# Three places of their own for the combined token operands, and a later ready time for them in the planner

## The chip, the core and the metric

One core of one Trainium2 chip runs the whole program. A core has TensorE (PE, matrix products into PSUM), VectorE (DVE), ScalarE (ACT), GpSimd (POOL) and SyncE (SP, which issues the transfers). The metric is the device time of one execution in microseconds (us), as a median of runs. All values are float32 at the interface.

## What is computed

```python
def reference(**kwargs):
    ...
    attn_out = _attn_ref(**attn_kwargs)     # two rounds of softmax attention over 4 x 8 heads, 576 tokens
    x = ...                                 # 2304 tokens x 512
    x = _moe_ref(x=x, **moe_kwargs)         # g = h*clip(h+3,0,6)/6 with h = x @ w_in;  g @ w_out
    return _moe2_ref(x=x, **moe2_kwargs)

def _moe2_ref(x, w_gate, w1, w2):
    ...
    for _ in range(8):                      # 8 rounds of row and column normalisation of P (2304 x 8)
        ...
    for e in range(E):                      # 8 experts
        h = np.maximum(x @ w1[e], 0.0)      # 512 -> 1024
        ye = h @ w2[e]                      # 1024 -> 512
        out += P[:, e:e + 1] * ye
```

The second mixture, `_moe2_ref`, takes three quarters of the time, and the change lies there.

## The kernel before, in words

**Stages.** 0 to about 140 us attention; then the first mixture (`layer1a`, `layer2a`); from about 375 to 525 us the gate and the normalisation of P (lines L1111 to L1190, small DVE instructions); the second mixture from about 440 us to the end. In the second mixture the 2304 tokens are six blocks of 384 (TB). A pair of blocks goes through all 32 groups of expert columns. The first pair (blocks 0 and 1) is pass 0, to about 944 us; the other two pairs share each group's weights in one long pass, from about 944 to 1946 us.

**Precision.** A float32 value is fed to TensorE as a high and a low part. `split_part` makes them: ACT copies the high part (L424), and the low part is the difference `x - high`, one tensor_tensor (L429) that may run on DVE or POOL. A product is three matmuls for each contraction chunk: high by high (L992), low by high (L993), high by low (L994).

**A unit** of the second mixture is one pair of token blocks and one group of columns. `layer1b` computes a 2 by 2 block product with seven products in place of eight. Its token operands a11, a12, a22, s1, s2, s3, s4 are made once for a pair by `operands` (L945): s1 = a21+a22, s2 = s1-a11, s4 = a12-s2, s3 = a11-a21 (L969, on DVE or POOL, for two halves c each), and each is then split. Its weight operands are made for each group by `combined` (L431): four differences of the raw weights (`m`, L451), and splits of them and of the raw weights: `w1h`, `w1l` and `w1xh`, `w1xl` (128x256 or 128x512 pieces). The weights of layer 2 are split whole: `w2h` on ACT and `w2l` (128x1024) on DVE or POOL.

Each product is six matmuls into a PSUM bank `ph`, about 1.04 us. A product's PSUM value is copied into a temporary `tmp` by ACT (L300) or DVE (L301), and DVE adds the next products to it with L1006, `u.t = ps.t + u.t`. In the order of a unit: a11 (copied), s3 (copied), s2 (copied into u2), a22, **L1006 (u2 += a22)**, s1, **L1006 (p7 += s1)**, a12, L1006 (p1 += a12), s4. The product s4 goes into the bank that s1 was in, so it waits until L1006 (p7 += s1) has read it. Then ACT applies relu (L1014), and the result is split into `hsh` (ACT, L424) and `hsl` (L429, DVE or POOL). `layer2b` (L1051 to L1053) follows in six groups of twelve matmuls into banks `po`, 1.36 us each, and DVE adds each to the output (L1075), times the share Pr. TensorE interleaves the units: part of the seven products of one unit stand beside products of the next unit, and layer 2 of the unit before stands between.

**What sets the order.** Nothing is issued in the order of the code. Every operation goes into a list scheduler (`Order`) that walks through the whole kernel before it is built. An operation has ways (engine and modelled cost), tiles that it holds, dependencies and a priority. `run` picks the operation that can start first, gives it the engine on which it ends first, and moves that engine's clock. The queues of the engines are what comes out. A tile needs a free place of its tag (`Res`): `place(tag, pool, count, late)` gives the count of places, and `late` is how many come on top for the second mixture. The model prices a DVE or POOL instruction by its columns alone, whatever the other engine does.

The result of an operation is ready for others at `o.end = start + cost + o.lat` plus 0.2 us; `lat` is 2.0 for transfers and otherwise 0. Operations with `lat` 0 and a priority of 100 or more have 0.2 us (PATIENCE) added in the comparison.

```python
    place("hs", hp, 3)
    place("tmp", hp, 2, 4)
```

The order that comes out is thus sensitive: a different free place or ready time at one operation moves those after it, on all engines, until the end of the program.

Of the kernel before, what the change touches and what calls it, by code (L numbers as in the profile page):

```python
# [133 lines left out]
def t_dve(n, fast=False):  # L134
    return 0.065 + n / (1920.0 if fast else 960.0)
# [6 lines left out]
def t_pool(n):  # L142
    return 0.15 + n / 465.0
# [7 lines left out]
def tile_kernel(  # L151
# [21 lines left out]
    E, _, F2 = moe2_w1.shape  # L173
# [6 lines left out]
    TB = 384  # L180
# [8 lines left out]
    def pool(name, stack=ctx, **kw):  # L189
        return stack.enter_context(tc.tile_pool(name=name, bufs=1, **kw))  # L190

    const, dp, accp, hp, wp = (pool(n) for n in ("const", "dp", "accp", "hp", "wp"))
# [8 lines left out]
    def place(tag, where, count, late=0):  # L201

        res[tag] = Res(count)
        res[tag].pool, res[tag].first, res[tag].late = where, count, late
# [20 lines left out]
        pieces[tag] += 1  # L225
        return tag if pieces[tag] % (len(res[tag].free_at) + len(extra)) < len(res[tag].free_at) else tag + "_early"
    place("hs", hp, 3)
    place("tmp", hp, 2, 4)
    place("ph", ph, 2, 2)
    place("po", ph, 2, 2)  # L230
    for j in range(NB):
# [33 lines left out]
    def maker(tag, shape, dt, parts):  # L265
        def make(i):
            r = res[tag]
            pool = r.pool if i < r.first else r.late_pool if i < r.first + r.late or not r.late else r.last_pool
            got = [pool.tile(shape, dt, tag=f"{tag}{x}_{i}", name=f"{tag}{x}_{i}") for x in parts]
            return got if len(parts) > 1 else got[0]  # L270

        return make

    def hold(tag, shape, dt=F32):
        return Hold(res[tag], maker(tag, shape, dt, ("",)))
# [30 lines left out]
    def alt(cost_dve, cost_pool, fn, spare=0.0, **kw):  # L306

        return order.op(
            [
                ("POOL", cost_pool, lambda: fn(nc.gpsimd)),  # L310
                ("DVE", cost_dve, lambda: fn(nc.vector), spare),
            ],
            **kw,
        )
# [106 lines left out]
    def split_part(dst, src, w, n, deps, prio, **kw):  # L421

        high = act(
            t_act(n), lambda: nc.scalar.activation(dst(w.t[0]), src(), AF.Copy),  # L424
            reads=deps, fills=[w], prio=prio, **kw,
        )
        return alt(
            t_dve(n), t_pool(n),
            lambda e: e.tensor_tensor(dst(w.t[1]), src(), as_f32(dst(w.t[0])), ALU.subtract),  # L429
            reads=deps, fills=[w], after=[high], prio=prio, spare=SPARE,  # L430
        )  # L431
# [50 lines left out]
    def operand():  # L482
        late = maker("xy", [128, KC // 2, TB], F32R, ("h", "l"))
        return Hold(
            res["xy"], lambda i: parts(two_of[i // 3], (i % 3) * KC * TB, (KC // 2, TB)) if i < 6 else late(i)
        )
# [336 lines left out]
    def tmp():  # L823
        return hold("tmp", [128, TB])
# [120 lines left out]
    def operands(pr, prio, after=lambda nth: ()):  # L945


        a, b = acc[2 * pr], acc[2 * pr + 1]
        o = {nm: operand() for nm in ("a11", "a12", "a22", "s1", "s2", "s3", "s4")}
        turn = {nm: after(n) for n, nm in enumerate(("a11", "a12", "a22", "s1", "s2", "s4", "s3"))}  # L950
        for nm, src, c0 in (("a11", a, 0), ("a12", a, 2), ("a22", b, 2)):
            for c in range(2):
                split_part(
                    lambda d, c=c: d[:, c, :], lambda src=src, c=c, c0=c0: src.t[:, c0 + c, :], o[nm], TB, [src],
                    prio - (nm == "a11"), after=turn[nm],
                )
        for c in range(2):
            s1, s2, s3, s4 = (tmp() for _ in range(4))
            a11, a12 = (lambda c=c: a.t[:, c, :]), (lambda c=c: a.t[:, 2 + c, :])
            a21, a22 = (lambda c=c: b.t[:, c, :]), (lambda c=c: b.t[:, 2 + c, :])  # L960
            for nm, s, i0, i1, how, deps in (
                ("s1", s1, a21, a22, ALU.add, [b]),
                ("s2", s2, lambda s1=s1: s1.t, a11, ALU.subtract, [s1, a]),
                ("s4", s4, a12, lambda s2=s2: s2.t, ALU.subtract, [a, s2]),
                ("s3", s3, a11, a21, ALU.subtract, [a, b]),
            ):
                alt(
                    t_dve(TB), t_pool(TB),
                    lambda e, s=s, i0=i0, i1=i1, how=how: e.tensor_tensor(s.t, i0(), i1(), how),  # L969
                    reads=deps, writes=[s], takes=[o[nm]], after=turn[nm], prio=prio,  # L970
                )
                split_part(
                    lambda d, c=c: d[:, c, :], lambda s=s: s.t, o[nm], TB, [s], prio
                )
        return o
# [232 lines left out]
    with tc.manual_schedule():  # L1208
# [25 lines left out]
        for gg in range(4):  # L1234
# [7 lines left out]
            writes=[wg], prio=90,  # L1242
# [21 lines left out]
        for blk in range(NB):  # L1264
            gate(blk)
        ops = {0: operands(0, 40)}
        routing()
        i = len(units)
        turn, done = 100 + G1, []
        for ps in passes:  # L1270
            for pr in ps:
                if pr not in ops:
                    ops[pr] = operands(
                        pr, 45 if pr > 1 else 200, lambda n, pr=pr: [done[-1] if pr > 1 else done[4 + 3 * n]]
                    )
            gs = list(range(G1, len(groups)))
            turns_of = [(gs[:2], pr) for pr in ps] + [([g], pr) for g in gs[2:] for pr in ps]
            ready = {}
            for some, pr in turns_of:
                for g in some:  # L1280
                    if g not in ready:
                        ready[g] = (*combined(g, turn), whole(g, "w2", turn, "w2"))
                        turn += 1
                for g in some:
                    wa, wb, w2 = ready[g]
                    hs = [pair("hs", [128, NFC, TB]) for _ in range(2)]
                    done.append(layer1b(i, ops[pr], wa, wb, hs))
                    for h in (1, 0):
                        layer2b(i, g, 2 * pr + h, w2, hs[h])
                    i += 1  # L1290
# [33 lines left out]
```

## Time and profile before

| | |
|---|---|
| time, median of 3 runs | 1957.03 us (1956.8 to 1957.29) |
| profiled execution, its own time | 1953.73 us, of which 1951.9 us are the profile's span |
| PE busy | 1915.4 us (98%) |
| DVE busy | 1208.9 us (62%) |
| ACT busy | 970.3 us (50%) |
| POOL busy | 947.6 us (49%) |

In the profile, L12 is line 12 of the kernel, and `out<-in` are tile names without their numbers. A timeline row is a start, a length, engine, line, operation and tiles; in square brackets stands how long the engine was idle before and what released it. "xN" at the end of a timeline row means N like instructions in a row, with their joint length. PE's rows overlap, since matmuls are pipelined: the next one starts while the last one is still shown. PEclk is the granted clock of TensorE as a share of 2.4 GHz.

### The profile page before, as it was taken

How to read it: one execution, taken by the hardware profiler on the slowest of the kernel's cores; microseconds unless marked ns; L12 is line 12 of the kernel's file. 1: busy time of each engine (PE TensorE's matmuls, PEld its weight loads, DVE VectorE, ACT ScalarE, POOL GpSimd, SP SyncE). 2: the span in 40 equal slices, each digit the busy share in tenths (PEclk: the TensorE clock that was granted, in tenths of full speed). 3: DMA queues.
4: the chain of work that ended last, by engine and by line, in shares of the span. 5: the costliest groups of instructions: out<-in, count | busy, mean ns of one | idle time of the engine just before them, and what ended most of it. 6: DMA issues, size and time to landing. Idle time of an engine off the chain costs nothing.

```text
span 1951.9 us, 28194 instructions
## 1 busy us (share of the span) xinstructions
PE 1915.4 (98%) x10573; PEld 1735.5 (89%) x10573; DVE 1208.9 (62%) x1998; ACT 970.3 (50%) x2135; POOL 947.6 (49%) x987
## 2 busy tenths in 40 slices
PE   6999999999999999999999999999999999999998
PEld 4789999999899989999899999999999999999997
DVE  6996686447866676666755655555555555555554
ACT  6885674335455555555554443444443344443432
POOL 2444675236665666656634544435344343444431
PEclk9999999999999999999999999999999999999999
DMA  9931121001222222222311101111110111101102
GB/s 212 190 91 33 51 70 44 11 1 44 66 65 72 69 65 76 65 65 65 87 33 33 44 22 44 33 33 33 33 44 33 33 33 33 44 22 44 33 11 66
DMA packets 103546, 104.87 MB, mean 54 GB/s; under 512 B 42736, under 2 KB 78576, under 8 KB 103408
## 3 DMA queue, kind: packets, MB, share of 16 engines
q1 hardware_dynamic: 103408, 103.06, 19.5%
q8 instruction: 83, 1.36, 0.3%
q14 instruction: 55, 0.45, 0.1%
HBM read 98.32 MB, written 4.72 MB: 53 GB/s over the span
## 4 chain that ended last, share of the span: by engine, by line
PE 91%; DVE 5%; ACT 1%; DMA 1%; issue 0%; POOL 0%; SPq 0%; DVEq 0%; ACTq 0%; POOLq 0%
PE po L1051 13%; PE po L1052 13%; PE po L1053 13%; PE ph L992 12%; PE ph L994 12%; PE ph L993 12%; PE po L924 3%; PE po L926 3%; PE po L925 3%; PE ph L886 2%; PE ph L888 1%; PE ph L887 1%; PE ph L837 1%; DMA k<-in_k_dram 1%; DVE m_early L344 0%
## 5 line engine op out<-in xcount | busy, mean ns | idle before, releaser
L1075 DVE SCALAR_TENSOR_TENSOR acc<-po,Pr,acc 128x512 f32<-128x512 f32 x504 | 377.2, 750 | 287.3 <-PE po L1053 284.0
L429 POOL TENSOR_TENSOR hsl<-tmp,hsh 128x384 fp32r<-128x384 f32 x382 | 392.5, 1032 | 325.2 <-ACT hsh L424 271.0
L1051 PE MATMUL po<-w2h,hsh 128*128 128x512 f32 x1152 | 448.9, 390 | 0.0
L1052 PE MATMUL po<-w2l,hsh 128*128 128x512 f32 x1152 | 448.7, 390 | 0.0
L1053 PE MATMUL po<-w2h,hsl 128*128 128x512 f32 x1152 | 448.6, 389 | 0.0
L429 POOL TENSOR_TENSOR w1xl<-m,w1xh 128x256 fp32r<-128x256 f32 x152 | 111.5, 756 | 321.6 <-ACT w1xh L424 321.6
L1053 PEld LDWEIGHTS po<-w2h,hsl 128*128 128x128 f32 x1152 | 216.2, 188 | 45.2
L300 ACT ACTIVATE tmp<-ph 128x384 f32<-128x384 f32 x241 | 117.9, 489 | 274.6 <-PE ph L994 263.3
L1051 PEld LDWEIGHTS po<-w2h,hsh 128*128 128x128 f32 x1152 | 216.3, 188 | 41.7 <-DVE acc L1075 0.2
L1052 PEld LDWEIGHTS po<-w2l,hsh 128*128 128x128 f32 x1152 | 216.3, 188 | 41.5
L424 ACT ACTIVATE hsh<-tmp 128x384 fp32r<-128x384 f32 x480 | 242.4, 520 | 20.2 <-DVE tmp L904 12.4
L1006 DVE TENSOR_TENSOR tmp<-ph,tmp 128x384 f32<-128x384 f32 x288 | 159.8, 556 | 147.3 <-PE ph L994 129.7
L424 ACT ACTIVATE w2h<-raw 128x1024 fp32r<-128x1024 f32 x64 | 67.9, 1061 | 350.2 <-PE po L1053 338.2
L1014 ACT ACTIVATE tmp<-tmp 128x384 f32<-128x384 f32 x288 | 149.7, 520 | 87.6 <-DVE tmp L1006 83.2
L992 PE MATMUL ph<-ax,w1h 128*128 128x384 f32 x448 | 151.5, 338 | 3.3 <-DVE tmp L1006 3.3
L994 PE MATMUL ph<-ax,w1l 128*128 128x384 f32 x448 | 150.7, 336 | 0.0
L993 PE MATMUL ph<-ax,w1h 128*128 128x384 f32 x448 | 150.5, 336 | 0.0
L429 DVE TENSOR_TENSOR hsl<-tmp,hsh 128x384 fp32r<-128x384 f32 x98 | 106.0, 1082 | 42.0 <-ACT hsh L424 38.5
L429 POOL TENSOR_TENSOR w1l<-raw,w1h 128x512 fp32r<-128x512 f32 (+1 forms) x104 | 116.1, 1130 | 7.0 <-ACT w1h L424 5.9
L451 POOL TENSOR_TENSOR m<-raw 128x256 f32<-128x256 f32 x58 | 44.5, 770 | 139.1 <-DMA raw<-in_moe_w_dram 136.3
L992 PE MATMUL ph<-xyh,w1h 128*128 128x384 f32 x320 | 108.3, 339 | 3.7 <-ACT tmp L300 3.7
L993 PE MATMUL ph<-xyl,w1h 128*128 128x384 f32 x320 | 108.1, 338 | 0.0
(207 smaller groups left out, 4035.7 us busy)
## 6 DMA issues: line engine op xcount, KB each, us to landing
raw<-in_moe_w_dram SPq DMA_DIRECT2D x128, 512.0 KB, 3.5
raw<-in_moe_w_in_dram SPq DMA_DIRECT2D x16, 512.0 KB, 3.8
raw<-in_moe_w_out_dram SPq DMA_DIRECT2D x16, 512.0 KB, 3.6
k<-in_k_dram SPq DMA_DIRECT2D x32, 144.0 KB, 5.9
q<-in_q_dram SPq DMA_DIRECT2D x32, 144.0 KB, 4.6
v<-in_v_dram SPq DMA_DIRECT2D x8, 576.0 KB, 6.7
out_dram<-acc SPq DMA_DIRECT2D x36, 128.0 KB, 2.4
p<-in_p_dram SPq DMA_DIRECT2D x1, 224.0 KB, 5.4
```

The source lines that it names most:

```text
L300: ("ACT", t_act(n, True), lambda: nc.scalar.activation(dst(), src(), AF.Copy)),
L424: t_act(n), lambda: nc.scalar.activation(dst(w.t[0]), src(), AF.Copy),
L429: lambda e: e.tensor_tensor(dst(w.t[1]), src(), as_f32(dst(w.t[0])), ALU.subtract),
L992: nc.tensor.matmul(out, wh[:, at + c, :], bh[:, c, :], start=first and c == 0, **on)
L993: nc.tensor.matmul(out, wh[:, at + c, :], bl[:, c, :], start=False, **on)
L994: nc.tensor.matmul(out, wl[:, at + c, :], bh[:, c, :], start=False, **on)
L1006: t_dve(n), lambda: nc.vector.tensor_tensor(u.t, ps.t[:, :n], u.t, ALU.add),
L1014: t_act(n, bool(ps)), lambda: nc.scalar.activation(c.t, src(), AF.Relu),
L1051: nc.tensor.matmul(ps.t, hh[:, f, ts], wh[:, f, :], start=(f == 0), stop=False)
L1052: nc.tensor.matmul(ps.t, hh[:, f, ts], wl[:, f, :], start=False, stop=False)
L1053: nc.tensor.matmul(ps.t, hl[:, f, ts], wh[:, f, :], start=False, stop=(f == NFC - 1))
L1075: lambda row=row, share=share, ps=ps: nc.vector.scalar_tensor_tensor(row(), ps.t, share(), row(), ALU.mult, ALU.add),
```

## The change

The six places of `tmp` in the second mixture become three, and three places with a new tag `st` are made; `operands` takes the combinations s1 to s4 from `st`. The four combinations carry `lat=2.0`, so the planner believes that they end 2 us later than they do.

```diff
     place("hs", hp, 3)
-    place("tmp", hp, 2, 4)
+    place("tmp", hp, 2, 1)
+    place("st", None, 0, 3)
     place("ph", ph, 2, 2)
...
         for c in range(2):
-            s1, s2, s3, s4 = (tmp() for _ in range(4))
+            s1, s2, s3, s4 = (hold("st", [128, TB]) for _ in range(4))
...
                 alt(
                     t_dve(TB), t_pool(TB),
                     lambda e, s=s, i0=i0, i1=i1, how=how: e.tensor_tensor(s.t, i0(), i1(), how),
-                    reads=deps, writes=[s], takes=[o[nm]], after=turn[nm], prio=prio,
+                    reads=deps, writes=[s], takes=[o[nm]], after=turn[nm], prio=prio, lat=2.0,
                 )
```

From the place of the diff on, line numbers of the changed kernel are one higher (L429 becomes L430, L1006 becomes L1007). No instruction of TensorE is added or removed. The queues of all engines are the same up to about 390 us. From there on, the order differs. DVE has 1973 rows in place of 1985, ACT 2117 in place of 2093, POOL 981 in place of 990.

On DVE, one unit of pass 0 (the one whose product a22 starts at 598.25 us in the trace of before; the numbers in a name are its place and a serial number). Before:

```order
L1075 SCALAR_TENSOR_TENSOR acc0_0_5526<-po_1_6889,Pr_0_5509,acc0_0_5526 128x512
L429 TENSOR_TENSOR w2l_0_6913<-raw_0_6833,w2h_0_6912 128x1024
L1006 TENSOR_TENSOR tmp_0_6931<-ph_2_6903,tmp_0_6931 128x384
L1006 TENSOR_TENSOR tmp_2_6922<-ph_0_6820,tmp_2_6922 128x384
L1006 TENSOR_TENSOR tmp_4_6844<-ph_3_6948,tmp_4_6844 128x384
L301 COPY tmp_3_6992<-ph_1_6971 128x384
L429 TENSOR_TENSOR hsl_0_6982<-tmp_1_6979,hsh_0_6981 128x384
```

Now:

```order
L1076 SCALAR_TENSOR_TENSOR acc0_0_5535<-po_1_6927,Pr_0_5522,acc0_0_5535 128x512
L1007 TENSOR_TENSOR tmp_0_6879<-ph_3_6835,tmp_0_6879 128x384
L430 TENSOR_TENSOR w1xl_1_6953<-m_1_6904,w1xh_1_6952 128x256
L1007 TENSOR_TENSOR tmp_2_6865<-ph_2_6809,tmp_2_6865 128x384
L430 TENSOR_TENSOR w1xl_1_6953<-m_0_6905,w1xh_1_6952 128x256
L430 TENSOR_TENSOR hsl_1_6968<-tmp_0_6879,hsh_1_6967 128x384
L430 TENSOR_TENSOR w1l_1_7003<-raw_1_6869,w1h_1_7002 128x512
```

The wide split `w2l` that stood ahead of the first L1006 has left DVE, and a split `w1xl` now stands between L1007 (u2 += a22) and L1007 (p7 += s1). This pattern comes 14 times in pass 0 now.

On POOL, the same unit now:

```order
L430 TENSOR_TENSOR hsl_2_6892<-tmp_1_6830,hsh_2_6891 128x384
L452 TENSOR_TENSOR m_1_6904<-raw_1_6869,m_2_6903 128x256
L430 TENSOR_TENSOR w2l_0_6943<-raw_0_6806,w2h_0_6942 128x1024
L430 TENSOR_TENSOR hsl_1_6968<-tmp_2_6865,hsh_1_6967 128x384
L430 TENSOR_TENSOR hsl_2_6892<-tmp_0_6991,hsh_2_6891 128x384
```

Here the wide split `w2l` stands, which needs `w2h` from ACT. And on ACT, the same unit now:

```order
L425 ACTIVATE w2h_0_6942<-raw_0_6806 128x1024
L425 ACTIVATE w1xh_1_6952<-m_1_6904 128x256
L425 ACTIVATE w1xh_1_6952<-m_0_6905 128x256
L1015 ACTIVATE tmp_0_6879<-tmp_0_6879 128x384
L425 ACTIVATE hsh_1_6967<-tmp_0_6879 128x384
```

`w2h` stands right ahead of the two `w1xh`, the first of which the first `w1xl` on DVE needs.

On DVE, where pass 0 ends and the operands of blocks 4 and 5 are made, the rows ahead of L1006 (p7 += s1), which is the last row of each piece. Before:

```order
L1075 SCALAR_TENSOR_TENSOR acc0_0_5526<-po_2_10432,Pr_0_5509,acc0_0_5526 128x512
L969 TENSOR_TENSOR tmp_0_10458<-acc5_0_3007 128x384
L969 TENSOR_TENSOR tmp_4_10468<-acc4_0_2867,acc5_0_3007 128x384
L1075 SCALAR_TENSOR_TENSOR acc0_0_5526<-po_3_10446,Pr_0_5509,acc0_0_5526 128x512
L969 TENSOR_TENSOR tmp_3_10484<-tmp_0_10458,acc4_0_2867 128x384
L429 TENSOR_TENSOR w1xl_1_10311<-m_1_10268,w1xh_1_10310 128x256
L1006 TENSOR_TENSOR tmp_1_10486<-ph_2_10352,tmp_1_10486 128x384
L969 TENSOR_TENSOR tmp_0_10502<-acc4_0_2867,tmp_3_10484 128x384
L1006 TENSOR_TENSOR tmp_2_10374<-ph_1_10339,tmp_2_10374 128x384
```

Now:

```order
L1076 SCALAR_TENSOR_TENSOR acc1_0_5569<-po_0_10413,Pr_0_5522,acc1_0_5569 128x512
L430 TENSOR_TENSOR ax0_94<-st_2_10387,ax0_94 128x384
L1076 SCALAR_TENSOR_TENSOR acc0_0_5535<-po_1_10430,Pr_0_5522,acc0_0_5535 128x512
L430 TENSOR_TENSOR w1l_1_10383<-raw_1_10240,w1h_1_10382 128x512
L970 TENSOR_TENSOR st_0_10466<-st_2_10387,acc4_0_2867 128x384
L1076 SCALAR_TENSOR_TENSOR acc0_0_5535<-po_2_10444,Pr_0_5522,acc0_0_5535 128x512
L1076 SCALAR_TENSOR_TENSOR acc0_0_5535<-po_3_10459,Pr_0_5522,acc0_0_5535 128x512
L970 TENSOR_TENSOR st_2_10493<-acc4_0_2867,st_0_10466 128x384
L1007 TENSOR_TENSOR tmp_0_10490<-ph_1_10352,tmp_0_10490 128x384
L430 TENSOR_TENSOR ax1_95<-st_0_10466,ax1_95 128x384
L1007 TENSOR_TENSOR tmp_2_10373<-ph_0_10340,tmp_2_10373 128x384
```

Before, four combinations (L969) and a `w1xl` stand among the last rows ahead of that L1006. Now it is two combinations, two splits `ax` of operands and a `w1l`, and the last accumulations of layer 2 stand closer to it.

## Rows read from the trace of the kernel before

**Rows 1.** The page, part 1: busy us (share of the span) xinstructions of each engine.

```profile
PE 1915.4 (98%) x10573; PEld 1735.5 (89%) x10573; DVE 1208.9 (62%) x1998; ACT 970.3 (50%) x2135; POOL 947.6 (49%) x987
```

**Rows 2.** Windows: per engine busy us (and matmul count), PEclk, DMA share, GB/s.

```profile
530.00:944.00 414.00, 414.00 (x2087) 375.53 (x2086) 281.08 (x407) 223.41 (x480) 256.04 (x274) 1.00 0.23 69
...
970.00:1946.00 976.00, 976.00 (x4919) 886.29 (x4919) 526.74 (x771) 413.08 (x878) 405.76 (x412) 1.00 0.12 34
```

**Rows 3.** Timeline of PE at its three waits after 460 us: start, length, [idle before <-releaser].

```profile
489.20 0.45 PE L992 MATMUL ph<-ax,w1h 128*128 128x384 f32 x1 [0.76 <-DVE tmp L1006]
...
526.05 0.45 PE L992 MATMUL ph<-ax,w1h 128*128 128x384 f32 x1 [2.52 <-DVE tmp L1006]
...
959.16 0.69 PE L992 MATMUL ph<-xyh,w1h 128*128 128x384 f32 x1 [3.66 <-ACT tmp L300]
```

**Rows 4.** Timeline of PE, one unit of pass 0: first matmul of its 1st and 4th product and of two layer-2 groups.

```profile
583.84 0.34 PE L992 MATMUL ph<-ax,w1h 128*128 128x384 f32 x1
...
586.96 0.34 PE L992 MATMUL ph<-ax,w1h 128*128 128x384 f32 x1
...
588.00 0.39 PE L1051 MATMUL po<-w2h,hsh 128*128 128x512 f32 x1
...
589.37 0.39 PE L1051 MATMUL po<-w2h,hsh 128*128 128x512 f32 x1
```

**Rows 5.** Timelines of ACT, DVE and POOL in the same unit.

```profile
584.04 1.06 ACT L424 ACTIVATE w2h<-raw 128x1024 fp32r<-128x1024 f32 x1 [0.59 <-PE po L1053]
...
585.08 0.56 DVE L1006 TENSOR_TENSOR tmp<-ph,tmp 128x384 f32<-128x384 f32 x1 [0.29 <-PE ph L994]
586.12 0.56 DVE L1006 TENSOR_TENSOR tmp<-ph,tmp 128x384 f32<-128x384 f32 x1 [0.48 <-PE ph L994]
...
585.18 2.42 POOL L429 TENSOR_TENSOR w2l<-raw,w2h 128x1024 fp32r<-128x1024 f32 x1 [0.89 <-ACT w2h L424]
```

**Rows 6.** Timelines of POOL and DVE: a vector instruction under a wide split, and one alone.

```profile
721.33 2.67 POOL L429 TENSOR_TENSOR w2l<-raw,w2h 128x1024 fp32r<-128x1024 f32 x1 [0.87 <-ACT w2h L424]
...
721.85 2.44 DVE L451 TENSOR_TENSOR m<-raw,m 128x256 f32<-128x256 f32 x1
...
670.18 0.41 DVE L429 TENSOR_TENSOR w1xl<-m,w1xh 128x256 fp32r<-128x256 f32 x1
```

**Rows 7.** Timelines of POOL and DVE before the wait at 488 us.

```profile
486.26 2.40 POOL L429 TENSOR_TENSOR w2l<-raw,w2h 128x1024 fp32r<-128x1024 f32 x1 [1.68 <-PE ph L1181]
...
487.07 1.62 DVE L1187 TENSOR_SCALAR ct<-ct 128x8 f32<-128x8 f32 x1
488.60 0.55 DVE L1006 TENSOR_TENSOR tmp<-ph,tmp 128x384 f32<-128x384 f32 x1
```

**Rows 8.** Timelines of POOL and DVE where a vector instruction isn't stretched.

```profile
458.51 1.44 POOL L429 TENSOR_TENSOR hsl<-tmp,hsh 128x384 fp32r<-128x384 f32 x1 [0.24 <-ACT hsh L424]
...
458.67 0.40 DVE L451 TENSOR_TENSOR m<-raw 128x256 f32<-128x256 f32 x1
```

**Rows 9.** Lines by shape, DVE and POOL, 530 to 944 us: busy us, mean ns | idle before.

```profile
L429 DVE TENSOR_TENSOR w2l<-raw,w2h 128x1024 fp32r<-128x1024 f32 x21 | 26.2, 1248 | 5.6 <-ACT w2h L424 5.5
...
L429 POOL TENSOR_TENSOR w2l<-raw,w2h 128x1024 fp32r<-128x1024 f32 x6 | 14.8, 2459 | 5.3 <-ACT w2h L424 5.3
```

**Rows 10.** Timeline of ACT ahead of the wait at 955 us, and windows around it.

```profile
957.73 0.99 ACT L424 ACTIVATE ax<-tmp 128x384 fp32r<-128x384 f32 x2 [4.84 <-DVE tmp L969]
958.63 0.47 ACT L300 ACTIVATE tmp<-ph 128x384 f32<-128x384 f32 x1
...
958.60:962.00 3.40, 2.84 (x9) 2.84 (x10) 3.40 (x5) 2.39 (x5) 3.16 (x3) 0.50 0.87 236
```

**Rows 11.** Timeline of DVE when the operands of blocks 4 and 5 are made.

```profile
945.47 1.65 DVE L969 TENSOR_TENSOR tmp<-acc 128x384 f32<-128x384 f32 x1
...
956.50 0.74 DVE L1075 SCALAR_TENSOR_TENSOR acc<-po,Pr,acc 128x512 f32<-128x512 f32 x1
```

**Rows 12.** Waits over the whole span: us in total, times, longest us.

```profile
ACT tmp L300 <- POOL hsl L429: 5.2, 17, 0.8
```

## The prediction, made before the changed kernel ran

> **What bounds the kernel now.** I read the page's busy shares first, then the windows by stage, then TensorE's timeline at its waits. TensorE is busy for 98% of the span [rows 1]. In pass 0 it is busy for 414.00 of 414.00 us and in the long pass for 976.00 of 976.00 [rows 2]. No other engine is near its limit: in pass 0 DVE has 281 and POOL 256 of 414 us [rows 2]. After 460 us TensorE waits three times: 0.76, 2.52 and 3.66 us [rows 3], together 6.94. Behind the third wait the clock stands at 0.50, its lower level, for 3.40 us with 2.84 us of PE busy [rows 10], so half of that, 1.4 us, is lost too. So the change can bring 8.3 us at most in this part, 0.4%. What it can cost isn't bounded: each wait that a new order makes in a full engine adds one for one.
>
> **Up to 390 us** the queues are alike, so attention and the first mixture cost the same. Three places for `tmp` in place of six could make a writer wait there, but not TensorE behind it: copies and relus have slack of a whole product.
>
> **Pass 0, the main term.** The change moves `w2l` of two units in four to POOL and in return `w1xl` to DVE: by the order, DVE has 35 `w1xl` in pass 0 where it had 4; before, 21 wide `w2l` stood on DVE and 6 on POOL [rows 9]. In 14 units a `w1xl` stands between L1006 (u2 += a22) and L1006 (p7 += s1), while POOL is to do a wide `w2l`. I take the unit of [rows 4, 5], where POOL has `w2l` at the same point but DVE has nothing between the two L1006. There the first product starts at 583.84 and s4 at 586.96, 3.12 us later, three products of 1.04 us [rows 4]. ACT makes `w2h` from 584.04 to 585.10, and POOL `w2l` from 585.18 to 587.60 [rows 5]. DVE's first L1006 starts at 585.08 and the second at 586.12, ending at 586.68, 0.28 us before s4 needs it [rows 4, 5]. So the cover of a `w1xl` is thin: 0.41 us alone [rows 6] would just fit into DVE's idle 0.48 us before the second L1006 [rows 5].
>
> It doesn't take 0.41 there. A DVE instruction that has only SBUF operands and starts inside a POOL tensor_tensor ends shortly after POOL does. At 721.85 an `m` of 128x256, the same shape, took 2.44 us; it ended at 724.29, 0.29 after the `w2l` that had started at 721.33 and took 2.67 [rows 6]. At 487.07 a scalar instruction on 128x8 took 1.62 and ended at 488.69, 0.03 after its `w2l` [rows 7]. L1006 itself, which reads PSUM, kept its 0.56 us inside a `w2l` [rows 5]. One row is against it: at 458.67 an `m` took 0.40 inside a POOL split [rows 8].
>
> The Trainium skill, GPSIMD Engine Reference, Key points, says that GpSimd shares its SBUF interfaces with VectorE and that they contend when the VectorE instruction has two SBUF inputs. The trace agrees for the two-input `m` [rows 6], and L1006 with one input from PSUM is untouched [rows 5]. The page gives no price.
>
> With that, step by step: the first L1006 starts at 585.08; `w1xl` starts behind it at about 585.6, inside `w2l`, and ends 0.29 after it, at 587.89. The second L1006 starts about 0.09 before that end, as L1006 at 488.60 did before 488.69 [rows 7], and ends 0.56 later, at 588.36. TensorE went on 0.05 us after such an L1006 (488.60 + 0.55 = 489.15, and 489.20) [rows 3, 7]. So s4 starts at 588.41 in place of 586.96: a wait of **1.45 us**. The clock stays, since after a wait of 2.52 it wasn't lower [rows 3]: the matmul there took 0.45 against 0.69 after the wait of 3.66. With `w2l` between 2.40 [rows 7] and 2.67 [rows 6] the wait is 1.43 to 1.70. Behind s4 comes layer 2 with nothing due, so nothing is won back: TensorE has no idle time there to give [rows 2]. Sum: 14 x 1.45 = **+20.3 us** (bounds 14 x 0 if nothing blocks, and 14 x 1.70 = 23.8).
>
> **Routing.** At 488 us the wait of 0.76 came from L1006 behind the stretched 128x8 instruction [rows 3, 7]. Now that L1006 stands ahead of it but behind a `w1xl`, again under a `w2l`: 1.45 by the same working, **+0.7** (0 to 0.9). The wait of 2.52 has six accumulations ahead of an L1006 in both orders and stays.
>
> **The step to the next pairs.** The wait of 3.66 goes: ACT's copy (L300) at 958.63 stood behind splits of combinations that had waited 4.84 us for DVE [rows 10], and now it doesn't. With the 1.4 us of clock that is 5.1. What is late next is L1006 (p7 += s1) in the DVE queue. From the start of layer 2 to that L1006 stand 19 vector instructions. Before, 12 such instructions (4 combinations, 4 accumulations, 4 splits) took from 945.47 to 956.50, 0.92 us each [rows 11], many stretched by POOL; 19 are 17.5 us. TensorE needs 6 x 1.37 for layer 2 and 4 x 1.04 for four products until s4 [rows 4], 12.4 us. So the wait is 5.1 at that pace, and none if they run unstretched. I take the middle, 2.5, since part of the splits has gone to POOL: **-2.6 us** (-5.1 to 0).
>
> **The long pass** has the same kinds of neighbours around L1006 on DVE in both orders, with the same period of four units; no new `w1xl` or other SBUF instruction stands between the two L1006 under a `w2l`. Cost 0. Its cover is the slack of the L1006; if it went, rival B says what it costs.
>
> **Sum:** 20.3 + 0.7 - 2.6 = +18.4 us. Against the profiled execution's own time, 1953.73, that is 1972.1. The median is 3.30 us higher, 1957.03, and what is measured is a median, so **1975.4 us**, 0.9% slower.
>
> **Rivals.**
>
> A, not slower: the two engines take turns instead of blocking, or `w1xl` starts just before `w2l` does and POOL is the one that is stretched. At half speed `w1xl` takes 0.82, from 585.6 to 586.4; L1006 ends at 586.9, and s4 at 586.96 is just in time. It decides at 0.9 us of `w1xl`. Then only the step to the next pairs is left: 1957.03 - 2.6 = 1954.4, and with the whole 5.1 us 1951.9. For it speaks [rows 8]; against it [rows 6, 7]. Advanced Engine Details and Errata of the Trainium skill, section VectorE Performance Modes, says that GpSimd and two-port VectorE instructions "will interfere/block eachother", which leaves both readings open; by turns the sum would be 1954.4, by blocking 1975.4.
>
> B, much slower: three places for `tmp` are too few. p1, p7 and u2 are held at once, and s4's relu needs a fourth until one is split. Then ACT's copy waits for the `hsl` that frees a place. With six places it waited for one 17 times, at most 0.8 us [rows 12]. A copy has one product, 1.04 us, less its own 0.47 [rows 4, 10], so 0.57 of cover; a wait of twice that, 1.1, costs 0.5 a unit. Over the 64 units of the long pass that is 32, and 2007 us. Against it: the planner counts the places, and it gave the long pass the same period.
>
> C, partly: ACT or a late transfer shifts `w2h`, so that `w2l` starts later than `w1xl` in half of the units. Then 7 x 1.45 = 10.2 in place of 20.3, and 1965.3.
>
> D, the change does nothing: the order after 390 us is another one, so only by accident.
>
> **Chances.** The forecast 0.65, A 0.15 (half of it within 0.2%, some of it faster), B 0.07, C 0.13. About 0.2% of the time, 3.9 us, is what a measurement of this kernel can tell from no change: 1953.1 to 1960.9. Faster takes the part of A in which the step gives nearly all: 0.05. Same takes the rest of A and the weakest of C: 0.12. Slower 0.83. The range leaves out B and the best of A: from 1954, A's middle, to 1982, the forecast with its upper bounds (23.8 + 0.9 - 0 = 24.7, 1981.7).
>
> **What would show it.** Right: 14 waits of about 1.45 us on TensorE in pass 0, each before the product s4, released by DVE's L1007, with a `w1xl` of about 2.3 us on DVE that ends with POOL's `w2l`; and PE idle at the step to the next pairs near 2.5 us with a full clock. Wrong: `w1xl` of 0.4 to 0.9 us in those places and no waits (A); waits of the copies on `hsl` through the long pass (B); or fewer or shorter waits because `w2l` comes late (C).

## The result

The changed kernel takes **1977.64 us** in the median (1975.15 to 1979.34) against 1956.91 us for the kernel before: a ratio of 1.0106, interval 1.0094 to 1.0118. It is slower by 20.7 us. The forecast was 1975.4 us. The profiled execution took 1975.15 us, of which 1973.4 are its span, 21.5 more than the span before. Two single executions among the runs below, 3868.77 us of lat_only and 10914.29 of before_halves (the one whose trace was kept), lie far above the rest and are left out of the ratios.

The page's busy row of after, beside [rows 1]:

```profile
PE 1918.9 (97%) x10573; PEld 1734.3 (88%) x10573; DVE 1238.0 (63%) x1986; ACT 975.4 (49%) x2158; POOL 935.6 (47%) x976
```

TensorE's work is the same, and its share has fallen to 97%. The windows by stage (columns as in [rows 2]; the last two stages begin later because of what was lost before them):

```profile
530.00:966.00 436.00, 417.98 (x2087) 374.99 (x2086) 316.63 (x433) 220.39 (x479) 244.23 (x246) 1.00 0.21 65
966.00:992.00 26.00, 23.34 (x117) 20.86 (x116) 22.30 (x27) 17.45 (x40) 23.02 (x20) 1.00 0.41 107
992.00:1967.00 975.00, 974.27 (x4909) 884.31 (x4909) 519.56 (x742) 418.65 (x894) 400.63 (x426) 1.00 0.12 34
```

In pass 0 PE was busy for 414.00 of 414.00 us [rows 2]; now 418.0 of 436. POOL does less there than before, DVE more. Nothing is near its limit: 18 us of PE idle time stand in a stage where DVE is idle for 119 us. One of the 14 units, with rows of ACT, DVE, POOL and PE of the timeline, to lay beside [rows 4, 5]:

```profile
603.73 1.06 ACT L425 ACTIVATE w2h<-raw 128x1024 fp32r<-128x1024 f32 x1 [6.36 <-PE po L1054]
...
604.84 0.56 DVE L1007 TENSOR_TENSOR tmp<-ph,tmp 128x384 f32<-128x384 f32 x1 [0.36 <-ACT w2h L425]
605.31 2.24 DVE L430 TENSOR_TENSOR w1xl<-m,w1xh 128x256 fp32r<-128x256 f32 x1
607.48 0.55 DVE L1007 TENSOR_TENSOR tmp<-ph,tmp 128x384 f32<-128x384 f32 x1
...
604.87 2.41 POOL L430 TENSOR_TENSOR w2l<-raw,w2h 128x1024 fp32r<-128x1024 f32 x1 [4.56 <-ACT w2h L425]
...
606.47 0.34 PE L995 MATMUL ph<-ax,w1l 128*128 128x384 f32 x1
608.08 0.44 PE L993 MATMUL ph<-ax,w1h 128*128 128x384 f32 x1 [1.26 <-DVE tmp L1007]
```

`w1xl` starts 0.44 us after `w2l` and ends at 607.55, 0.27 after it; 2.24 us for an instruction that takes 0.41 alone [rows 6]. L1007 (p7 += s1) is next on DVE and ends at 608.03, and PE starts s4 at 608.08. The last matmul had started at 606.47 and the next would have followed 0.17 later, so s4 is 1.44 us late. The idle time of 1.26 in brackets is less because a matmul's row is longer than its step. The same wait stands 14 times, 1.25 or 1.26 us each. The waits and lines of after in numbers (waits: us in total, times, longest; lines: busy us, mean ns | idle before):

```profile
PE ph L993 <- DVE tmp L1007: 25.4, 19, 2.7
...
ACT tmp L301 <- DVE hsl L430: 29.6, 41, 1.9
...
ACT tmp L301 <- POOL hsl L430: 9.5, 9, 1.3
```

```profile
L430 DVE TENSOR_TENSOR w1xl<-m,w1xh 128x256 fp32r<-128x256 f32 x35 | 44.9, 1281 | 1.3 <-ACT w1xh L425 1.3
...
L430 DVE TENSOR_TENSOR w2l<-raw,w2h 128x1024 fp32r<-128x1024 f32 x13 | 15.9, 1224 | 4.1 <-ACT w2h L425 4.1
...
L430 POOL TENSOR_TENSOR w2l<-raw,w2h 128x1024 fp32r<-128x1024 f32 x14 | 33.6, 2401 | 39.3 <-ACT w2h L425 39.3
```

35 `w1xl` on DVE take 1281 ns in the mean. The counts of `w2l` have moved from 21 and 6 [rows 9] to 13 and 14.

Four other places where PE waited, DVE, POOL and PE of each in turn (a fifth, a wait of 0.40 us near 786 us, comes up in the part on the prediction). At 488 us:

```profile
485.49 2.65 DVE L430 TENSOR_TENSOR w1xl<-m,w1xh 128x256 fp32r<-128x256 f32 x1
...
485.47 2.39 POOL L430 TENSOR_TENSOR w2l<-raw,w2h 128x1024 fp32r<-128x1024 f32 x1
...
488.67 0.45 PE L993 MATMUL ph<-ax,w1h 128*128 128x384 f32 x1 [1.45 <-DVE tmp L1007]
```

At the step to the next pairs:

```profile
980.67 2.12 DVE L970 TENSOR_TENSOR st<-acc,st 128x384 f32<-128x384 f32 x1
...
979.99 2.38 POOL L430 TENSOR_TENSOR w2l<-raw,w2h 128x1024 fp32r<-128x1024 f32 x1
...
984.25 0.45 PE L993 MATMUL ph<-xyh,w1h 128*128 128x384 f32 x1 [2.66 <-DVE tmp L1007]
```

In the long pass, once:

```profile
1104.34 2.63 DVE L452 TENSOR_TENSOR m<-raw,m 128x256 f32<-128x256 f32 x1
...
1104.24 2.45 POOL L430 TENSOR_TENSOR w2l<-raw,w2h 128x1024 fp32r<-128x1024 f32 x1 [1.22 <-ACT w2h L425]
...
1107.95 0.45 PE L993 MATMUL ph<-xyh,w1h 128*128 128x384 f32 x1 [0.73 <-DVE tmp L1007]
```

And behind the six DVE instructions (L1070) near 523 us, PE alone:

```profile
525.65 0.69 PE L993 MATMUL ph<-ax,w1h 128*128 128x384 f32 x1 [2.52 <-DVE tmp L1007]
526.13 0.52 PE L994 MATMUL ph<-ax,w1h 128*128 128x384 f32 x1
526.46 0.52 PE L995 MATMUL ph<-ax,w1l 128*128 128x384 f32 x1
```

Three of the four have a SBUF instruction on DVE that lasted until the end of POOL's `w2l`: a `w1xl` of 2.65 us, a combination (L970) of 2.12 and an `m` (L452) of 2.63. The hold isn't special to these rows. Among the rows that stand singly in this trace, from 260 us on, 23 `w1xl` and 83 `hsl` start on DVE under a POOL instruction and early enough to end there. None does: the `w1xl` (128x256) end 0.27 to 0.29 us behind POOL's instruction, the `hsl` (128x384) 0.40 to 0.43 behind it.

At the fourth place the wait is the 2.52 us of before [rows 3], but the clock is at its lower level behind it (PEclk 0.50 from 525.6 to 528.8): the matmuls are 0.52 long, where those of [rows 4] are 0.34, and they start 0.31 to 0.33 apart in place of 0.17.

### The profile page after: what moved, and what is told of

Its sections match the earlier page's. It is cut to its first block, busy times and chain, and to the rows that moved or that the text cites. A ratio compares the mean times of both kernels' runs of the same rounds, so it can differ in the third digit from the quotient of the medians.

```text
span 1973.4 us, 28291 instructions
## 1 busy us (share of the span) xinstructions
PE 1918.9 (97%) x10573; PEld 1734.3 (88%) x10573; DVE 1238.0 (63%) x1986; ACT 975.4 (49%) x2158; POOL 935.6 (47%) x976
## 4 chain that ended last, share of the span: by engine, by line
PE 87%; DVE 8%; ACT 2%; issue 1%; DMA 1%; POOL 1%; SPq 0%; DVEq 0%; POOLq 0%; ACTq 0%
PE po L1052 13%; PE po L1053 13%; PE po L1054 13%; PE ph L993 11%; PE ph L995 11%; PE ph L994 11%; PE po L925 3%; PE po L927 3%; PE po L926 3%; DVE w1xl L430 2%; PE ph L887 2%; PE ph L889 1%; PE ph L888 1%; DVE tmp L1007 1%; PE ph L838 1%
## 5 line engine op out<-in xcount | busy, mean ns | idle before, releaser
L430 POOL TENSOR_TENSOR hsl<-tmp,hsh 128x384 fp32r<-128x384 f32 x381 | 390.5, 1030 | 340.2 <-ACT hsh L425 315.8
L301 ACT ACTIVATE tmp<-ph 128x384 f32<-128x384 f32 x264 | 126.5, 487 | 296.6 <-PE ph L995 254.6
L430 POOL TENSOR_TENSOR w1xl<-m,w1xh 128x256 fp32r<-128x256 f32 x150 | 111.5, 762 | 307.7 <-ACT w1xh L425 307.6
L1007 DVE TENSOR_TENSOR tmp<-ph,tmp 128x384 f32<-128x384 f32 x288 | 159.2, 554 | 141.5 <-PE ph L995 138.9
L430 DVE TENSOR_TENSOR hsl<-tmp,hsh 128x384 fp32r<-128x384 f32 x99 | 102.9, 1040 | 73.3 <-ACT hsh L425 70.6
L430 POOL TENSOR_TENSOR w2l<-raw,w2h 128x1024 fp32r<-128x1024 f32 x33 | 79.4, 2407 | 73.7 <-ACT w2h L425 73.7
L993 PEld LDWEIGHTS ph<-ax,w1h 128*128 128x128 f32 x448 | 84.4, 188 | 28.5 <-DVE tmp L1007 27.4
L993 PE MATMUL ph<-ax,w1xh 128*128 128x384 f32 x320 | 108.0, 337 | 0.0
```

Of the source, the lines that this page charges most:

```text
L301: ("ACT", t_act(n, True), lambda: nc.scalar.activation(dst(), src(), AF.Copy)),
L993: nc.tensor.matmul(out, wh[:, at + c, :], bh[:, c, :], start=first and c == 0, **on)
L1007: t_dve(n), lambda: nc.vector.tensor_tensor(u.t, ps.t[:, :n], u.t, ALU.add),
```

## The experiments

Theory **T1**: the `w1xl` is held until POOL's instruction ends, and the L1007 behind it releases PE late. Theory **P1**: it is the places, not the later ready time, that make this order. Rivals stand in the expectations. Ratios are against the kernel before, run on the same chip in the same rounds, with 95% intervals.

**1. The order of two instructions.** On DVE the second L1007 is issued ahead of the `w1xl`, in 15 places, and nothing else moves:

```diff
-            fn()
+            self.emit(o, eng, fn)
...
+            if eng == "DVE" and o.kind == "plus":
+                fn()
+                held[1]()
...
+        if eng == "DVE" and o.kind == "w1xl" and self.last == "plus" and self.phase:
+            self.held = (o, fn)
+            return
```

> The changed kernel, with one thing altered: where a split w1xl stands on DVE right between two L1007 rows, the second L1007 is issued first and the w1xl behind it (15 places, the 14 of pass 0 and the one at 488 us). All other queues are the same. Theory T1 (the w1xl is blocked under POOL's w2l and holds back the second L1007): the 14 waits of PE of 1.26 us and the one of 1.45 are gone, 14 x 1.5 + 0.7 = 21.7 us less, about 1956 against 1977.6. Theory T2 (POOL and ACT work is in the way whatever DVE's order is, and the L1007 is late because the unit as a whole is late): the waits stay within 0.3 us each, 1974 to 1978.

Measured: **1959.26 us**, ratio 1.0019 (1.0009 to 1.0028). DVE in the same unit, and PE's waits on L1007 (here L1029) over the span:

```profile
604.65 0.56 DVE L1029 TENSOR_TENSOR tmp<-ph,tmp 128x384 f32<-128x384 f32 x1 [0.41 <-PE ph L1017]
605.13 1.61 DVE L452 TENSOR_TENSOR w1xl<-m,w1xh 128x256 fp32r<-128x256 f32 x2
...
PE ph L1015 <- DVE tmp L1029: 6.9, 6, 2.6
...
PE ph L1204 <- DVE cs L1199: 1.5, 1, 1.5
```

The second L1029 now waits only for PE's product (0.41 idle), and both `w1xl` come behind it. 19 waits of 25.4 us in all have become 6 of 6.9 us. T1 holds, T2 falls. The gain is 18.4 us, not the 21.7 expected. A wait of 1.5 us now stands at 495 us, at a small instruction of the normalisation (L1204 <- L1199); four short waits of 0.23 to 0.41 us stand in pass 0; and the clock falls to its lower level behind the wait of 2.65 us at 967 us (PEclk 0.50 from 968.5 to 971.0), where the changed kernel kept it behind 2.66.

**2. The length of POOL's instruction.** The wide `w2l` on POOL is issued as two instructions of half the width; every queue keeps its order:

```diff
-            lambda e: e.tensor_tensor(dst(w.t[1]), src(), as_f32(dst(w.t[0])), ALU.subtract),
+            if e is nc.gpsimd and n == 1024 and len(dst(w.t[1]).shape) == 2:
+                parts = [(0, n // 2), (n // 2, n)]
...
+            for i, j in parts:
+                e.tensor_tensor(dst(w.t[1])[:, i:j], src()[:, i:j], as_f32(dst(w.t[0]))[:, i:j], ALU.subtract)
```

> The changed kernel, with each wide split w2l that POOL does issued as two instructions of 128x512 in place of one of 128x1024; no other row moves. Theory T1 (a DVE instruction on SBUF is held until the running POOL instruction ends): the w1xl that starts 0.44 us behind w2l now ends with the first half, at about 1.24 + 0.29 = 1.53 us in place of 2.41 + 0.29 = 2.70 after w2l began. Each wait of PE is 1.17 us shorter, 0.1 to 0.3 in place of 1.26 idle; 14 x 1.2 = 16.8 and some 1 us at 488 and at 1107 less, about 1960. If POOL's second half goes first where both wait, the w1xl ends as late as before, and the time stays at 1977. Theory T3 (POOL and DVE share a path by turns, and w1xl is slow in proportion to the work that runs beside it): the same work runs beside it, waits stay over 1.0 us, 1974 to 1978.

Measured: **1957.98 us**, ratio 1.0008 (0.9999 to 1.0018). A unit's DVE, POOL and PE rows, and the lines of pass 0:

```profile
601.31 1.14 DVE L433 TENSOR_TENSOR w1xl<-m,w1xh 128x256 fp32r<-128x256 f32 x1
602.37 0.55 DVE L1015 TENSOR_TENSOR tmp<-ph,tmp 128x384 f32<-128x384 f32 x1
602.84 1.04 DVE L433 TENSOR_TENSOR w1xl<-m,w1xh 128x256 fp32r<-128x256 f32 x1
...
600.86 2.73 POOL L435 TENSOR_TENSOR w2l<-raw,w2h 128x512 fp32r<-128x512 f32 x2 [4.56 <-ACT w2h L425]
...
602.97 0.44 PE L1001 MATMUL ph<-ax,w1h 128*128 128x384 f32 x1 [0.16 <-DVE tmp L1015]
```

```profile
L433 DVE TENSOR_TENSOR w1xl<-m,w1xh 128x256 fp32r<-128x256 f32 x35 | 36.4, 1039 | 0.0
...
L435 POOL TENSOR_TENSOR w2l<-raw,w2h 128x512 fp32r<-128x512 f32 x28 | 38.2, 1387 | 38.6 <-ACT w2h L425 38.6
```

The `w1xl` ended at 602.45, 1.59 us after `w2l` began (1.53 expected), though POOL's two halves together took 2.73, more than the whole had (2.41). The first half ended at 602.16, 0.29 before the `w1xl` did. Each of the 14 waits is 0.15 or 0.16 us. POOL's work on `w2l` was the same in sum, and half of it was still to do when the `w1xl` ended; what counted was where an instruction on POOL ends. That rules out T3, and with it rival A. The next `w1xl` (602.84) was held under the second half instead, where nobody waited. One wait grew: the one of 0.40 us near 786 us is 1.14 here, at 776.67. There DVE's wide `w2l` (774.02) starts 0.15 us behind a POOL instruction (773.87) and takes 1.67 us; in the changed kernel it started 0.13 us ahead of POOL's and took 1.21.

**3. One half of the change, and the other.** The later ready time alone:

```diff
-                    reads=deps, writes=[s], takes=[o[nm]], after=turn[nm], prio=prio,
+                    reads=deps, writes=[s], takes=[o[nm]], after=turn[nm], prio=prio, lat=2.0,
```

> The kernel before with half of the change: the combinations count as ready 2 us later, tmp keeps its six places, and there is no st. Its order has no w1xl between two L1006 under a w2l in pass 0. If the new places are what makes the order with the 14 waits (P1): no such waits, 1953 to 1961. If the later ready time makes it (P2): about 1977.

Measured: **1954.27 us**, ratio 0.9989 (0.9979 to 0.9999). And the places alone:

```diff
-    place("tmp", hp, 2, 4)
+    place("tmp", hp, 2, 1)
+    place("st", None, 0, 3)
```

> The changed kernel with the other half alone: three places for tmp and three for st, without the 2 us. Its order has 13 places with a w1xl between two L1007 under a w2l. P1 (the places make the waits): 13 x 1.5 = 19.5 us of waits in pass 0, and an unknown step to the next pairs (waits of 0 to 5 us there); 1971 to 1981. P2 (the 2 us make them): 1953 to 1961.

Measured: **1978.77 us**, ratio 1.0118 (1.0102 to 1.0133). PE's waits on DVE's additions, the later ready time first, then the places:

```profile
PE ph L992 <- DVE tmp L1006: 5.9, 4, 2.5
```

```profile
PE ph L993 <- DVE tmp L1007: 24.4, 20, 3.5
```

4 waits against 20, and 13 of the 20 are the waits of 1.25 or 1.26 us in pass 0, as many as the order had places for them. P1 holds: the places make the order that costs. Whether it is the fewer places of `tmp` or the separate ones of `st` wasn't tried. Taken alone, the 2 us bring a little, if anything.

**4. How many SBUF inputs.** The `w1xl` that DVE does become copies of one input:

```diff
-            lambda e: e.tensor_tensor(dst(w.t[1]), src(), as_f32(dst(w.t[0])), ALU.subtract),
+            lambda e: (e.tensor_copy(dst(w.t[1]), src()) if e is nc.vector and kw.get("lone") else e.tensor_tensor(dst(w.t[1]), src(), as_f32(dst(w.t[0])), ALU.subtract)),
```

> The changed kernel; the w1xl pieces that DVE does are a copy of one SBUF input in place of the difference of two (the low part of these weights is therefore not the reference's). All queues keep their order. If a DVE instruction is held under POOL's w2l only when it reads two SBUF inputs (T4): a copy of 128x256 takes 0.2 to 0.45 us there, the 14 waits vanish, about 1957. If one with a single SBUF input is held as well (T5, as the 128x8 instruction of one input at 487.07 us in the kernel before was): the copies take about 2.2 us, the waits stay at 1.2 to 1.3 us, 1974 to 1979.

Measured once: 1975.86 us. DVE and POOL in a unit, and PE's waits over the span:

```profile
606.14 2.11 DVE L430 CAST w1xl<-m 128x256 fp32r<-128x256 f32 x1
...
608.64 0.28 DVE L430 CAST w1xl<-m 128x256 fp32r<-128x256 f32 x1
...
605.70 2.41 POOL L430 TENSOR_TENSOR w2l<-raw,w2h 128x1024 fp32r<-128x1024 f32 x1 [4.56 <-ACT w2h L425]
...
PE ph L993 <- DVE tmp L1007: 22.9, 19, 2.6
```

The copy needs 0.28 us alone, and 2.11 under `w2l`, ending 0.14 after it. The 14 waits are 1.12 or 1.13 us, a little under the range expected. So a copy with one input is held as well (T5). That fits the GPSIMD Engine Reference of the Trainium skill, Key points, only if this copy runs in a two-port mode; the trace doesn't show the mode.

**5. A planner that knows of the hold.** In the changed kernel a split or combination isn't given to DVE while POOL's instruction has over 1 us to go:

```diff
+                    if eng == "DVE" and o.sbuf and self.phase and self.pool[0] < s < self.pool[1] - 1.0:
+                        s = self.pool[1]
```

> The changed kernel with a planner that knows of the hold: in the second mixture a split or combination isn't put on DVE while POOL's current instruction has over 1 us to go; it is given the start at that instruction's end. Its order has no w1xl between two L1007 under a w2l any more. T1: the 14 waits vanish; what the new order does at 488, 523 and at the step to the next pairs isn't known, 0 to 10 us there; 1950 to 1962. If the waits come from the three places: the places are the same, 1970 to 1980.

Measured: **1957.56 us**, ratio 1.0008 (0.9999 to 1.0017). PE's waits on DVE's additions:

```profile
PE ph L1000 <- DVE tmp L1014: 8.8, 5, 3.6
```

The three places are kept, and the 14 waits are gone (five others are left, one of them the step to the next pairs). So the places don't force the waits: the order that the planner chose with them made them. That the places cost nothing isn't shown, since the rule changes the whole order, and with six places the 2 us alone were at 0.9989.

**6. A faster version.** The later ready time with the halves, then with quarters, the halves on the kernel before, and the halves with the planner's rule:

> The kernel before with the later ready time alone, and POOL's wide w2l in two instructions. By T1 all waits behind a SBUF instruction under a w2l shrink by about 1.2 us: the wait of 0.77 at 488 goes, the one of 2.52 at 523 falls to about 2.0, the one of 2.10 at 957 to 1 or 2; 1950 to 1953. If the halves cost POOL time that somebody waits for: 1955 to 1960.

> As lat_halves, with four instructions of 128x256 in place of two. T1: the longest hold falls to about 0.75 us, nothing is left of it; 1949 to 1953. If each more instruction on POOL costs a start of 0.1 us or more and delays what stands behind it: 1953 to 1957.

> The kernel before, with nothing altered but POOL's wide w2l in two instructions. T1: of its three waits, the one of 0.76 at 488 goes (its L1187 ends with the first half), the one of 2.52 at 523 loses some 0.5, the one of 3.66 at 955 has other causes and stays: 0.8 to 1.5 us less, 1954.5 to 1956. If lat_halves owes its gain to the halves alone, this is as fast as it, 1952.5; if to the later ready time alone, 1956.

> lat_halves with the planner that keeps splits off DVE while POOL's instruction has over 1 us to go. T1: the planner still takes w2l for one instruction of 2.4 us, so it moves work for a hold that the halves have already cut; waits like those of lat_halves (0.7 to 6 us in all after 450 us), 1950 to 1956. If the two add up: 1950 or less.

Measured: **1952.42** (0.9982, 0.9973 to 0.9992), 1952.54 (0.9986, 0.9976 to 0.9995), 1953.39 (0.9990, 0.9980 to 0.9999) and 1953.33 us (0.9988, 0.9978 to 0.9997). All four are faster than the kernel before by 0.1 to 0.2%, and their intervals overlap, so which part brings most can't be told. Quarters bring no more than halves, and the rule adds nothing to the halves. The halves alone were 1.1 us faster than their range had it. What is left in lat_halves (waits over the whole span):

```profile
PE ph L999 <- DVE tmp L1013: 5.3, 3, 2.7
```

As expected, the wait at 488 us is gone and the one near 523 us is 1.99. The longest, 2.67 us near 957, was to be 1 to 2.

## Why the prediction was right, step by step

**The mechanism** was right: a `w1xl` held under `w2l` between two L1006. The second L1007, a SBUF and PSUM instruction behind it, starts 0.07 us before its end (607.48, 607.55), much as [rows 7] had shown (0.09).

**The main term** was +20.3 (14 x 1.45). Measured: 14 waits, with s4 1.44 us late. But the step is larger by 0.1 than the working had it: the first matmul after a wait takes 0.44, and the next one follows 0.28 later in place of 0.17 (608.08 and 608.36 in PE's timeline). The trace of before shows this (489.20 is 0.45 long [rows 3]), and the prediction didn't read it. So 1.55 a unit. The start of the same matmul in the two traces shows it: between 530 and 944 us of before, the shift grows by 21.9, of which 0.6 belong to another wait (below): 21.3, or 1.52 for each of the 14.

**Routing**, +0.7: the wait was 0.76 [rows 3] and is 1.45. Right.

**The wait of 2.52 "stays", and "the clock stays"**: the wait did stay, the clock didn't. Behind it the first step took 0.48 us (0.29 in the kernel before), and nine steps of 0.31 to 0.33 followed in place of 0.17, until 529.01; that loses 1.6 us. The step that failed rested on one row. Here a term was missing.

**The step to the next pairs**, -2.6: a wait of 2.66 with an unbroken clock in place of 3.66 and 1.4 of clock. The shift falls by 2.5 between 944 and 1000 us. The middle of the bounds was taken for a wait of 2.5, and that this came close is luck: the working reckoned with many small stretches, but 1.6 of the 2.66 us come from one combination, which took 2.12 us under a `w2l` where one like it takes 0.54 (at 984.12).

**The long pass**, 0: one wait of 0.73 at 1107.95, with the slower start behind it 1.0 us. The prediction looked for SBUF instructions between the two L1006; here an `m` of 2.63 stood ahead of all three. A wait of 0.40 in pass 0 near 786 us, where two L1007 stood behind a `w2l` on DVE, was missed too (0.6).

**The sum.** 21.3 + 0.7 + 1.6 - 2.5 + 1.0 + 0.6 = 22.7. The attention and the first mixture, whose queues are alike, were 1.2 us shorter in this execution (the same matmul near 300 us started that much earlier), which leaves 21.5, as between the spans. The forecast of +18.4 was short by the slower start behind each wait, the clock and the two small waits, 4.2 us in all, of which the 1.2 hid a part. Between the medians the difference is 20.7.

**The rivals.** A fell with the lengths of `w1xl` and with experiment 2. The row that spoke for it [rows 8] fits a hold the other way round: POOL's `hsl` is 1.44 us long there, where the median of its like rows is 1.02, so POOL lost about the 0.40 that DVE's `m` took. B's mechanism exists: ACT's copies (L301) now wait 41 times (33 of them in the long pass), up to 1.9 us, for DVE's `hsl` that frees a place of `tmp`, where the kernel before had 17 such waits, on POOL's `hsl`, of 0.8 at most [rows 12]. But PE never waits for such a copy, so the cover held and B fell. C fell: the 14 waits are alike within 0.01 us. D fell with the 20.7 us.

## What to carry to other kernels

Where DVE and GpSimd share work, a long GpSimd instruction held the differences of two SBUF tensors that began on DVE under it until it ended (2.24 us in place of 0.41), and with it all that was queued behind; look for what stands ahead of the one DVE instruction that TensorE waits for, not at busy shares. Two cheap cures worked here: cut the long instruction in two (1957.98 us), or let the planner keep such work off DVE meanwhile (1957.56, against 1977.64). Where a list scheduler sets the order, read what a change of places or ready times does to the queues before running it: here the queue alone, with durations from the old trace, gave the loss within 3 us.

## What the runs showed of the hardware that was not expected

- **The clock behind a wait of 2 to 2.7 us isn't set by the wait's length alone.** After 2.52 us it stayed at full speed in the kernel before [rows 3] and in lat_only; after 2.52 it fell to its lower level in the changed kernel, and in swap a moment later. After 2.66 it stayed in the changed kernel, but it fell after 2.65 in swap, after 2.16 in halves and after 2.10 in lat_only. Such a fall cost 1.6 us in the changed kernel. What else decides was not tried. Windows of about 3 us around the ends of such waits, two of the changed kernel and two of halves (the first of these behind a wait of 1.99; columns as in [rows 2]; PEclk is the third number from the end):

```profile
525.10:528.60 3.50, 2.95 (x9) 2.95 (x10) 2.02 (x4) 2.75 (x6) 1.86 (x3) 0.57 0.00 0
983.70:987.00 3.30, 2.75 (x16) 2.75 (x17) 1.94 (x4) 3.24 (x9) 2.42 (x3) 1.00 0.97 308
```

```profile
524.90:528.40 3.50, 3.00 (x17) 3.00 (x18) 2.08 (x4) 2.66 (x7) 2.10 (x3) 1.00 0.00 0
966.80:970.00 3.20, 2.70 (x11) 2.70 (x12) 2.47 (x3) 2.66 (x7) 2.02 (x3) 0.76 0.96 296
```

- **A plain copy with one SBUF input is held as well**: 2.11 us against 0.28 (experiment 4). But not every such instruction is: in the kernel before, inside the very `w2l` of POOL that held the 128x8 scalar instruction for 1.62 us [rows 7], a reciprocal of 128x8, which reads and writes the same tag, had just kept its 0.20 us:

```profile
486.83 0.20 DVE L1186 RECIPROCAL ct<-ct 128x8 f32<-128x8 f32 x1
```
